# Moving the start-up work of a fused attention and gated-MLP kernel: one load queue, an earlier copy, later transposes, no power function on GpSimd

## The chip, the cores and the metric

The kernel runs on one NeuronCore of one Trainium2 chip. The metric is device microseconds of one execution, as the median of several; lower is better. Besides the time, each execution has a *span*: from the first to the last instruction that the profile records. The time is longer than the span.

In the profile the engines are PE (TensorE matmuls), PEld (TensorE weight loads), DVE (VectorE), ACT (ScalarE), POOL (GpSimd) and SP (SyncE, which here only issues DMAs). A "q" behind a name means the engine's sequencer, for instance the time in which it issues a DMA.

## The reference

The input x is normalised once (layer norm without scale), and two branches use the result: a sliding dilated local attention and a gated bilinear MLP. Cut to what matters:

```python
# x: 2048 x 640 bf16; 32 heads of 20; window 8, dilation 2; F = 1536
xn  = (x - mean) / sqrt(var + 1e-5)
qkv = xn @ wqkv                              # 640 x 1920
attn over the 8 keys at pos, pos-2, ..., pos-14
A   = attn_output @ wo
B   = ((xn @ w_gate) * (xn @ w_up)) @ w_down
return x + A + B
```

## The kernel before

Every operation goes through a small scheduler: the program calls `op(engine, ...)` in one sequence, each engine runs its share in that order, and the scheduler adds the semaphore waits. So the order of the calls is the order on each engine; nothing is reordered.

The sixteen row tiles of x (128 x 640) are loaded, normalised and transposed. Tiles 0 to 3 are transposed by TensorE and copied out of PSUM, tiles 4 to 15 by DMA ("transposing loads" below). Q and K of tiles 0 to 3 are projected tile by tile with 128-wide matmuls, of tiles 4 to 7 with 256-wide ones, and everything after that with 512-wide ones.

The loads, alternating between the queues of SP and ScalarE:

```python
    x_load(1, "act")
    x_load(0)
    for c in range(NCH):                                  # NCH = 5: the Q weights
        wqkv_load(0, c, ("sp", "act")[c % 2])
    x_load(2, "act")
    x_load(3)
    for c in range(NCH):                                  # the K weights
        wqkv_load(1, c, ("sp", "act")[c % 2])
    for t in range(4, 8):
        x_load(t)
```

The layer norm of tile t. For tiles 8 to 15 the reciprocal root comes from GpSimd:

```python
    def ln_aggr(t):
        ...
        op("dve", ... bn_aggr(mv, st) ...)                # mean, variance
        if t >= 8:
            op("pool", ... tensor_scalar(sd, mv[:, 1:2], EPS, None, op0=ALU.add) ...)
            op("pool", ... tensor_tensor(rstd, sd, NEGH[:, 0:1], ALU.pow) ...)   # NEGH = -0.5
            return
        op("act", ... activation(sd, mv[:, 1:2], ACT.Sqrt, bias=EPSC[:, 0:1]) ...)

    def ln_apply(t):
        ...
        if t < 8:
            op("dve", ... reciprocal(rstd, sd) ...)
        op("dve", ... tensor_scalar(xs, x, mean, rstd, subtract, multiply) ...)
        if t >= NTP:                                      # NTP = 4
            op("sp", ... dma_start_transpose(XNT tile t, xs) ...)
        if t + 8 < NT:
            x_load(t + 8)
```

The start. `warm` issues matmuls on zeros, `ln_pe` the five PE transposes of a tile, `ln_copy` the copies of the transposed tile from PSUM to SBUF (half by ScalarE, half by VectorE for tiles 0 and 1):

```python
    warm(10)
    ln_stats_a(0); ln_stats_b(0); ln_aggr(0)
    ln_stats_a(1)
    ln_apply(0)
    ln_pe(0)
    ln_stats_b(1)
    ln_aggr(1)
    ln_copy(0)
    ln_apply(1)
    ln_stats_a(2)
    warm(2)
```

The transposes of tiles 1 to 3 are put between the projections' groups of five matmuls, one group for each of the five row blocks c of the weights. The key is (Q or K, tile), the value the group ahead of which the transpose stands:

```python
    at = {(0, 0): (3, lambda: tr(1)), (0, 1): (4, lambda: tr(2)), (1, 1): (2, lambda: tr(3))}
```

## Time and profile before

| | before |
|---|---|
| time | 255.28 us (255.06 to 255.30, 3 runs) |
| span of the profiled execution | 253.7 us (that execution took 255.53 us) |
| PE busy | 249.7 us, 98% |
| first projection matmul / first 512-wide one | 6.72 / 30.48 us |
| last matmul begins | 251.12 us |

From the page of before: the span, the engines' busy times, and the engines' shares of the chain that ended last.

```profile
span 253.7 us, 3853 instructions
PE 249.7 (98%) x1573; PEld 149.3 (59%) x1573; DVE 216.5 (85%) x241; ACT 112.9 (45%) x202; POOL 47.0 (19%) x73
PE 95%; DMA 2%; DVE 1%; ACTq 0%; ACT 0%; issue 0%
```

PE sets the time. Its waits in the whole execution of before (who waited for whom: us in total, times, longest):

```profile
PE PS L420 <- DVE EPSC L298: 1.0, 1, 1.0
PE PS L403 <- DVE XNS L389: 0.3, 1, 0.3
PE PS L468 <- ACT XNT L414: 0.2, 1, 0.2
```

The first is the wait before the very first matmul. The other two, about 0.5 us, are all that PE loses later: the transposes of tile 2 wait for its normalised rows (XNS), and the first projection waits for ScalarE's copy of transposed tile 0 (XNT). The chain of waits of before says why tile 2 is late (start, us, what):

```profile
2.36 5.57 DMA XST<-in_A_x_dram
...
7.95 0.49 DVE STATS L358
8.45 0.19 DVE XNT L412
8.63 0.41 DVE STATS L364
...
9.84 0.46 DVE XNS L389
10.30 0.05 issue
10.34 0.45 PE PS L403 x5
```

Tile 2's load is issued at 2.36 us and lands at 7.93; VectorE's in-order chain of statistics and normalisation follows. VectorE's copy of transposed tile 1 (8.45) also stands behind that load. From 10.34 us to the last matmul the chain is PE alone.

The power function, in the timelines of GpSimd and VectorE of before (start, us, what, and in brackets the idle time before it and who ended it):

```profile
21.73 0.22 POOL L373 TENSOR_SCALAR SD<-MV 128x1 f32<-128x1 f32 x1 [1.22 <-DVE MV L370]
22.03 0.58 POOL L374 TENSOR_TENSOR SD<-SD,NEGH 128x1 f32<-128x1 f32 x1
22.64 0.45 DVE L389 TENSOR_SCALAR XNS<-XST,MV,SD 128x640 bf16<-128x640 bf16 x1 [0.65 <-POOL SD L374]
```

VectorE waits for GpSimd in each of these eight tiles, 5.5 us in total (0.65 us here, 1.0 us at the last). PE does not wait for that.

```profile
q1 hardware_dynamic: 144, 0.04, 4.2%
q14 instruction: 1, 0.01, 0.8%
```

### The profile page before, as it was taken

The numbers are of one execution on the slowest core, as the hardware profiler recorded it, in microseconds if no ns is written. First come the engines' busy times: TensorE is split into PE (matmuls) and PEld (weight loads), VectorE is DVE, ScalarE is ACT, GpSimd is POOL, SyncE is SP. The second block draws the span as 40 slices with busy tenths as digits, with TensorE's granted clock in tenths as the row PEclk, the third lists the DMA queues.
The fourth block names the chain that finished last, engine by engine and source line by source line (L and its number), as shares of the span: only waits on it lengthen the run. The fifth ranks groups of instructions, "written<-read, shape, count | busy, mean of one in ns | idle before, by whom it ended". The sixth has DMA issues, their size and how long they took to land.

```text
span 253.7 us, 3853 instructions
## 1 busy us (share of the span) xinstructions
PE 249.7 (98%) x1573; PEld 149.3 (59%) x1573; DVE 216.5 (85%) x241; ACT 112.9 (45%) x202; POOL 47.0 (19%) x73
## 2 busy tenths in 40 slices
PE   8999999999999999999999999999999999999996
PEld 3899955555554444444444447764444777777775
DVE  5896679999999994999999994899999999995221
ACT  3575557555555557555555553325555112211000
POOL 2003320113453252002232102120000112112000
PEclk9999999999999999999999999999999999999999
DMA  6959448967866546364469962393000042332311
GB/s 213 332 117 170 82 79 303 375 178 142 138 127 110 106 83 125 114 238 90 75 117 253 393 230 24 51 314 68 3 0 0 4 50 26 36 45 26 80 52 52
DMA packets 25665, 31.84 MB, mean 126 GB/s; under 512 B 10000, under 2 KB 22160, under 8 KB 25616
## 3 DMA queue, kind: packets, MB, share of 16 engines
q1 hardware_dynamic: 18448, 21.31, 26.7%
q0 software_dynamic: 6336, 9.31, 23.7%
q10 hardware_dynamic: 864, 0.98, 1.2%
q8 instruction: 12, 0.20, 0.3%
q14 instruction: 5, 0.04, 0.0%
HBM read 14.42 MB, written 4.59 MB: 75 GB/s over the span
## 4 chain that ended last, share of the span: by engine, by line
PE 95%; DMA 2%; DVE 1%; ACTq 0%; ACT 0%; issue 0%
PE PS L614 41%; PE PS L645 29%; PE PS L442 17%; PE PS L475 4%; PE PS L457 2%; DMA XST<-in_A_x_dram 2%; PE PS L468 1%; DVE STATS L358 0%; ACTq L294 0%; PE PS L403 0%; ACT L321 0%; DVE XNS L389 0%; DVE STATS L364 0%; DVE FOUT L654 0%; DVE MV L370 0%
## 5 line engine op out<-in xcount | busy, mean ns | idle before, releaser
L614 PE MATMUL PS<-XNT,WG 128*128 128x512 bf16 x240 | 59.6, 379 | 0.0
L614 PE MATMUL PS<-XNT,WU 128*128 128x512 bf16 x240 | 59.6, 379 | 0.0
L581 DVE TENSOR_TENSOR PVB<-VO,ATB 128x10240 f16<-128x10240 bf16 x8 | 43.9, 5489 | 0.2
L442 PE MATMUL PS<-XNT,WQKV 128*128 128x512 bf16 x200 | 43.3, 379 | 0.0
L645 PE MATMUL PS<-WD,HT 128*128 128x320 bf16 (+1 forms) x300 | 43.2, 294 | 0.0
L614 PEld LDWEIGHTS PS<-XNT,WU 128*128 128x128 bf16 x240 | 23.5, 98 | 28.3
L614 PEld LDWEIGHTS PS<-XNT,WG 128*128 128x128 bf16 x240 | 23.5, 98 | 28.2
L616 ACT ACTIVATE USX<-PS 128x512 bf16<-128x512 f32 x48 | 28.7, 597 | 22.6 <-PE PS L614 22.2
L645 PEld LDWEIGHTS PS<-WD,HT 128*128 128x128 bf16 x300 | 28.7, 98 | 10.9
L442 PEld LDWEIGHTS PS<-XNT,WQKV 128*128 128x128 bf16 x200 | 23.5, 118 | 19.4
L576 DVE TENSOR_TENSOR PVB<-PVB 128x5120 f16<-128x5120 f16 (+1 forms) x16 | 34.5, 2156 | 0.3
L509 POOL DMA_DIRECT2D LOG<-PE x24 | 22.5, 937 | 57.6 <-DMA LOG<-PE 57.4
L649 ACT ACTIVATE FACC<-PS 128x320 f16<-128x320 f32 x24 | 10.5, 437 | 41.9 <-PE PS L645 41.9
L616 ACT ACTIVATE HT<-PS 128x512 bf16<-128x512 f32 x36 | 21.5, 597 | 16.5 <-PE PS L614 16.5
L645 PE MATMUL PS<-WO,VO 128*128 128x320 bf16 (+1 forms) x165 | 27.1, 295 | 0.0
L660 POOL DMA_DIRECT2D out_dram<-FACC x12 | 10.4, 865 | 71.2 <-ACT FACC L649 71.2
L645 PEld LDWEIGHTS PS<-WO,VO 128*128 128x128 bf16 x165 | 15.9, 98 | 5.9
L498 DVE TENSOR_TENSOR TMP<-QH,KH 128x2048 f16<-128x2048 bf16 x16 | 19.1, 1218 | 0.0
L498 DVE TENSOR_TENSOR PP<-QH,KH 128x2048 f16<-128x2048 bf16 x16 | 18.9, 1218 | 0.0
L503 DVE TENSOR_TENSOR PP<-PP,TMP 128x4096 f16<-128x4096 f16 x8 | 18.3, 2291 | 0.2
L654 DVE TENSOR_TENSOR FOUT<-PS,XR 128x320 bf16<-128x320 f32 (+1 forms) x9 | 4.1, 455 | 15.8 <-PE PS L645 15.8
L449 ACT ACTIVATE VO<-PS 128x512 bf16<-128x512 f32 x20 | 11.9, 597 | 9.6 <-PE PS L442 9.6
(65 smaller groups left out, 227.8 us busy)
## 6 DMA issues: line engine op xcount, KB each, us to landing
PE<-PP POOLq DMA_DIRECT2D x8, 512.0 KB, 4.8
ATB<-LOG SPq DMA_DIRECT2D x8, 512.0 KB, 4.3
LOG<-PE POOLq DMA_DIRECT2D x24, 128.0 KB, 2.7
XST<-in_A_x_dram SPq DMA_DIRECT2D x14, 160.0 KB, 4.7
WG<-in_B_w_gate_dram SPq DMA_DIRECT2D x1, 1920.0 KB, 9.4
WU<-in_B_w_up_dram SPq DMA_DIRECT2D x1, 1920.0 KB, 16.1
WD<-in_B_w_down_dram SPq DMA_DIRECT2D x1, 1920.0 KB, 10.3
out_dram<-in_A_x_dram SPq DMA_DIRECT2D x1, 1920.0 KB, 10.1
```

The lines of the kernel that those rows point to most:

```text
L442: op("pe", (lambda l, x, c: lambda e: e.matmul(PS[:, b, :], l, x, start=(c == 0), stop=(c == NCH - 1)))(l, x, c), r=[l, x], w=[PS[:, b, :] ...
L449: op("act", lambda e: e.activation(o, PS[:, b, :], ACT.Copy, scale=sc), r=[PS[:, b, :]], w=[o], name=f"pev{which}_{m}_{j}")
L498: return (1.22, lambda: op("dve", lambda e: e.tensor_tensor(o, qw, kw, ALU.mult), r=[q, k], w=[o], name=f"prod{h}_{p}_{c}"))
L503: (2.3, lambda: op("dve", lambda e: e.tensor_tensor(a, a, b, ALU.add), r=[a, b], w=[a], name=f"psum{h}_{p}")),
L509: op("pool", lambda e: e.dma_start(o, i, accum_op=ALU.add), r=[o, i], w=[o], dma=True, name=name)
L576: return lambda: op("dve", lambda e: e.tensor_tensor(o, x, y, ALU.add), r=[x, y], w=[o], name=f"{name}_{b}")
L581: lambda: op("dve", lambda e: e.tensor_tensor(PVB[:], vw, aw, ALU.mult), r=[v, a], w=[PVB[:]], name=f"pv_{b}")),
L614: op("pe", (lambda l, x, c: lambda e: e.matmul(PS[:, b, :], l, x, start=(c == 0), stop=(c == NCH - 1)))(l, x, c), r=[l, x], w=[PS[:, b, :] ...
L616: op("act", lambda e: e.activation(o, PS[:, b, :], ACT.Copy), r=[PS[:, b, :]], w=[o], name=f"guev{which}_{m}_{j}")
L645: op("pe", (lambda l, x, i, b: lambda e: e.matmul(PS[:, b, 0:wid], l, x, start=(i == 0), stop=(i == n - 1)))(l, x, i, b), r=[l, x], w=[PS[ ...
L649: op("act", (lambda o, b: lambda e: e.activation(o, PS[:, b, 0:wid], ACT.Copy))(o, b), r=[PS[:, b, :]], w=[o], name=f"fin{t}_{nb}")
L660: stores.append(op("pool", lambda e: e.dma_start(d, f, accum_op=ALU.add), r=[f, ("out",)], w=[("out", t)], dma=True, name=f"oacc{t}"))
```

## The change

Four edits, meant to shorten the first 11 us and to free GpSimd of the small operations of layer norm: (1) all weight loads and tile 2 on SP's queue; (2) ScalarE's copy of transposed tile 0 ahead of the Sqrt of tile 1, which waits for statistics; (3) the PE transposes of tiles 1 to 3 later among the projections; (4) no pow: tiles 8 to 15 use ScalarE's Sqrt and VectorE's reciprocal, as tiles 0 to 7 do.

```diff
-    NEGH = sb("NEGH", [128, 16], FP32)
-    op("pool", lambda e: e.memset(NEGH[:], -0.5), w=[NEGH[:]], name="negh")
     for c in range(NCH):
-        wqkv_load(0, c, ("sp", "act")[c % 2])
-    x_load(2, "act")
+        wqkv_load(0, c)
+    x_load(2)
     x_load(3)
     for c in range(NCH):
-        wqkv_load(1, c, ("sp", "act")[c % 2])
+        wqkv_load(1, c)
@@ ln_aggr
-        if t >= 8:
-            rstd = SD[:, t, 1:2]
-            op("pool", ... tensor_scalar ... add ...)
-            op("pool", ... tensor_tensor ... pow ...)
-            return
@@ ln_apply
-        if t < 8:
-            op("dve", lambda e: e.reciprocal(rstd, sd), ...)
+        op("dve", lambda e: e.reciprocal(rstd, sd), ...)
@@ ln_copy gets an argument `only`, to emit one engine's copy alone
@@ start
     ln_pe(0)
+    ln_copy(0, "act")
     ln_stats_b(1)
     ln_aggr(1)
-    ln_copy(0)
+    ln_copy(0, "dve")
@@ projections
-    at = {(0, 0): (3, lambda: tr(1)), (0, 1): (4, lambda: tr(2)), (1, 1): (2, lambda: tr(3))}
+    at = {(0, 0): (4, lambda: tr(1)), (1, 0): (3, lambda: tr(2)), (1, 1): (4, lambda: tr(3))}
```

More of the change, by code (lines that the diff above doesn't have):

```diff
@@ L370, in ln_aggr @@
         op("dve", lambda e: e.bn_aggr(mv, st), r=[st, ("stb", t)], w=[mv], name=f"bnag{t}")
-        if t >= 8:
-            rstd = SD[:, t, 1:2]
-            op("pool", lambda e: e.tensor_scalar(sd, mv[:, 1:2], EPS, None, op0=ALU.add), r=[mv], w=[("sd", t)], name=f"sd{t}")
-            op("pool", lambda e: e.tensor_tensor(rstd, sd, NEGH[:, 0:1], ALU.pow), r=[("sd", t), NEGH[:]], w=[("rstd", t)],
-               name=f"rstd{t}")
-            return
         op("act", lambda e: e.activation(sd, mv[:, 1:2], ACT.Sqrt, bias=EPSC[:, 0:1]), r=[mv, EPSC[:]], w=[("sd", t)],
@@ L384, in ln_apply @@
         sd, rstd = SD[:, t, 0:1], SD[:, t, 1:2]
-        if t < 8:
-            op("dve", lambda e: e.reciprocal(rstd, sd), r=[("sd", t)], w=[("rstd", t)], name=f"rstd{t}")
+        op("dve", lambda e: e.reciprocal(rstd, sd), r=[("sd", t)], w=[("rstd", t)], name=f"rstd{t}")
         for c0, c1 in ((0, 2 * 128), (2 * 128, D)) if t == 0 else ((0, D),):
@@ L403, in ln_pe, with ln_copy @@
             op("pe", (lambda o, i: lambda e: e.transpose(o, i, IDENT[:]))(o, i), r=[i, IDENT[:]], w=[o], name=f"tr{t}_{c}")
-    def ln_copy(t):
+    def ln_copy(t, only=None):
         parts = ((("act", 0, 2), ("dve", 2, NCH)), (("dve", 0, 2), ("act", 2, NCH)), (("act", 0, NCH),),
@@ L408, in ln_copy @@
         for eng, c0, c1 in parts:
+            if only is not None and eng != only:
+                continue
             o = XNT[:, c0:c1, t * TS:(t + 1) * TS]
```

## The prediction

> **What bounds it.** TensorE: busy 98% of the 253.7 us span, clock granted in full; the chain of waits is 95% PE. From tile 2's transposes at 10.34 us to the last matmul at 251.36 that chain is PE without a wait, so only the first 11 us can give anything back. PE's waits there: 0.98 us before the warming matmuls, 0.18 us on ScalarE's copy of transposed tile 0 (first projection matmul at 6.72), 0.34 us on VectorE's normalised tile 2 (10.00 to 10.34). The weight-load row adds 0.26 us (until 8.69) behind VectorE's copy of tile 1, about 0.2 us for PE. Together 0.7 us.
>
> Tile 2 is late because its statistics wait for its x load, issued at 2.36, landed at 7.93, eighth to land. The DMA share is 1.0 (340 to 380 GB/s) from 5 to 10.8 us: bandwidth-bound, not issue-bound.
>
> **What the change does.**
> - *One queue.* An issue costs 0.43 to 0.46 us, so thirteen on SP end near 6.7 us instead of 4.9. The landing order (two x tiles, five Q weights, tiles 2 and 3, K weights) is already that of the trace. [...]at 164 KB per 0.455 us (360 GB/s) one queue nearly keeps up. Tile 2 lands at 7 to 8 us.
> - *Copy before second Sqrt.* ScalarE's copy starts when its transposes end, near 5.6 instead of 6.30; PE's 0.18 us wait goes. But VectorE's copy of tile 1 sits behind tile 2's statistics, so if tile 2 still lands at 7.93, the wait ending near 8.69 grows by as much.
> - *Later transposes.* Tile 2's go behind 20 more matmuls (0.057 us each): the 0.34 us wait vanishes. Tile 1's behind five more: 0 to -0.1. Tile 3's behind ten more: copied near 14.0, needed near 15.
> - *No pow.* Sixteen GpSimd instructions (224 and 569 ns) go; eight Sqrt on ScalarE (0.29 us) and reciprocals on VectorE (0.16 us) come. VectorE's tile period falls from 2.09 to 1.65 us (the 0.64 us waits on GpSimd go), so layer norm ends about 3.5 us earlier, near 32. PE does not wait for that. ScalarE's evacuations now stand behind Sqrts paced by VectorE and lag up to 3.5 us; with eight PSUM banks filled at 1.09 us each, over 2 us remain before PE would stall. Tile 11's transposing load lands near 27.5 instead of 29.7, which keeps the other gains from being eaten.
>
> **Sum.** PE reaches the 200 wide-row matmuls 0.5 us earlier (0.3 to 0.8). All after that is PE-paced and moves as a block.
>
> Predicted 254.7 us, 80% range 253.9 to 255.5. Chances: faster by over 2% 0.01, within 2% 0.97, slower 0.02.
>
> **Right if:** no PE wait on ScalarE's copy near 6.6 nor on tile 2's normalisation; 512-wide projections start near 30.0 instead of 30.48; VectorE's first 2048-wide product near 32 instead of 35.55; PE's busy time per group equal; ScalarE waits more on VectorE's statistics, without a PE wait from it. A remaining PE wait near 8.5 on VectorE's copy shows whether tile 2 landed sooner.
>
> **Wrong if:** one queue delivers clearly slower (tile 2 or K weights after 9 or 10 us: PE waits on WQKV), or ScalarE's lag exhausts the PSUM banks (PE waits on ScalarE between 20 and 40 us): up to 2 us slower. Or earlier VectorE work shifts the DMA accumulations and stalls PE later.

Cut from the step *One queue* is a statement about several issuing queues that no run here shows. It was no term of the sum: the sum, 0.5 us (0.3 to 0.8), and the 254.7 us made from it are whole. What carries that step is the estimate from the trace, 164 KB per 0.455 us of issue, against a mean of 362 GB/s that the DMA of before moved from 5 to 10.8 us.

## More of the kernel before

One view that I looked at only afterwards belongs here as well: the DMA queues in two stretches of before. First 140 to 149 us, then 252 to 256 us, which is the very end. Queues q8 and q14 carry instruction fetches; the columns are packets, MB, and the packets' time as a share of 16 DMA engines.

```profile
q8 instruction: 1, 0.02, 0.7%
q14 instruction: 2, 0.02, 0.4%
```

## The result, and the profile after

| | before | after |
|---|---|---|
| time, median | 255.22 us (255.06 to 255.34, 6 runs) | 255.38 us (255.32 to 259.66, 6 runs) |
| span of the profiled execution | 253.7 us | 253.0 us |
| first 512-wide matmul | 30.48 us | 29.77 us |
| last matmul begins | 251.12 us | 250.40 us |

The ratio is 1.0009, with a 95% interval from 0.9996 to 1.0023: the same. Ratios here are the mean time of one kernel's fast runs over that of the other's of the same rounds, so they are not quite the ratio of the medians quoted. One of the six runs of after (259.66 us, clock 0.993) was slow and is left out.

The page of after, the same lines:

```profile
span 253.0 us, 3850 instructions
PE 249.6 (99%) x1573; PEld 149.6 (59%) x1573; DVE 218.1 (86%) x249; ACT 114.0 (45%) x210; POOL 41.0 (16%) x56
PE 99%; DVE 0%; issue 0%
```

PE's waits of after, all of them:

```profile
PE PS L413 <- DVE EPSC L297: 1.0, 1, 1.0
```

The chain of waits of after, from the start into the tile-wise projections, has PE alone. (The chain counts a piece from the end of the one before it, so its times lie a little behind the starts quoted elsewhere: 6.83 us here, 6.62 us in the timeline.)

```profile
0.99 4.45 PE PS L413 x10
5.44 0.53 PE PS L394 x5
5.98 0.85 PE PS L413 x2
6.83 1.12 PE PS L461 x20
7.95 0.28 PE PS L394 x5
8.23 2.65 PE PS L461 x45
```

Inside the span of this execution nearly everything went as foreseen: both waits are gone, PE has no wait after its first matmul, and all that follows is 0.7 us earlier (predicted 0.5, within 0.3 to 0.8). VectorE's layer norm ends at 32.0 us, where it ended at 35.6. In the timelines of ScalarE and VectorE of after, ScalarE's evacuations now stand behind a Sqrt that waits for VectorE, and they lag; for that reason VectorE's first product of the attention starts at 33.37 us and not at 32 as I had written:

```profile
24.43 0.29 ACT L369 ACTIVATE SD<-MV,EPSC 128x1 f32<-128x1 f32 x1 [0.87 <-DVE MV L368]
24.64 0.36 ACT L476 ACTIVATE QH<-PS 128x256 bf16<-128x256 f32 x1
33.37 1.23 DVE L491 TENSOR_TENSOR PE<-QH,KH 128x2048 f16<-128x2048 bf16 x1 [1.35 <-ACT KH L476]
```

PE does not wait for any of it. And yet the time is not shorter. The profiled execution of after took 255.32 us with a span of 253.0, a difference of 2.3 us; that of before took 255.53 us with 253.7, a difference of 1.8. The six runs of after all have 2.26 to 2.34 us. So about half a microsecond had appeared *outside* the span. That was the question for the experiments.

### The profile page after: what moved, and what is told of

It reads as the page before. It is cut to its first block, busy times and chain, and to the rows that moved or that the text cites. A ratio compares the mean times of both kernels' runs of the same rounds, so it can differ in the third digit from the quotient of the medians.

```text
span 253.0 us, 3850 instructions
## 1 busy us (share of the span) xinstructions
PE 249.6 (99%) x1573; PEld 149.6 (59%) x1573; DVE 218.1 (86%) x249; ACT 114.0 (45%) x210; POOL 41.0 (16%) x56
## 4 chain that ended last, share of the span: by engine, by line
PE 99%; DVE 0%; issue 0%
PE PS L607 41%; PE PS L638 29%; PE PS L435 17%; PE PS L468 4%; PE PS L461 2%; PE PS L450 2%; PE PS L413 2%; PE PS L394 1%; DVE FOUT L647 0%; DVE ZERO L296 0%; DVE EPSC L297 0%
## 5 line engine op out<-in xcount | busy, mean ns | idle before, releaser
L502 POOL DMA_DIRECT2D LOG<-PE x24 | 21.9, 925 | 58.4 <-DMA LOG<-PE 58.1
```

The source lines that it names most:

```text
L502: op("pool", lambda e: e.dma_start(o, i, accum_op=ALU.add), r=[o, i], w=[o], dma=True, name=name)
```

## The experiments

All ran in five rounds against before on the same chip. "Copy", "slots", "queue" and "pow" are the four edits. Runs of one table block share the runs of before. The spans are to 0.1 us, so only the first decimal of "time minus span" counts.

| run | what it is | time, median | ratio, 95% interval | spans of its runs | time minus span |
|---|---|---|---|---|---|
| *(before, first)* | 11 runs | 255.65 | | 253.2 to 254.8 | 1.77 to 1.88, one 2.09 |
| c_before | before again | 255.78 | 0.9995 (0.9976 to 1.0014) | 253.3 to 254.1 | 1.76 to 1.82 |
| c_after | after again | 255.55 | 1.0007 (0.9983 to 1.0032) | 253.1 to 254.8 | 2.23 to 2.28 |
| e_twoq | after, two queues | 255.44 | 0.9992 (0.9970 to 1.0014) | 252.5 to 254.0 | 2.27 to 2.34 |
| e_pow | after, with pow | 254.80 | 0.9986 (0.9954 to 1.0019) | 252.8 to 255.1 | 1.76 to 1.83 |
| *(before, second)* | 11 runs | 255.32 | | 253.2 to 254.0 | 1.78 to 1.85 |
| p4_gps | after + 4 idle GpSimd memsets | 256.36 | 1.0031 (1.0012 to 1.0050) | 253.3 to 255.2 | 1.74 to 1.83 |
| p17_dve | after + 17 idle VectorE memsets | 255.31 | 0.9998 (0.9985 to 1.0011) | 252.8 to 253.2 | 2.27 to 2.31 |
| o_nopow | before, pow removed | 256.10 | 1.0030 (1.0018 to 1.0042) | 253.7 to 254.0 | 2.27 to 2.30 |
| p4_twoq | e_twoq + 4 idle GpSimd memsets | 254.92 | 0.9984 (0.9971 to 0.9997) | 252.8 to 253.6 | 1.77 to 1.82 |
| *(before, third)* | 11 runs | 255.41 | | 253.3 to 254.0 | 1.76 to 1.85 |
| o_oneq | before, one queue | 255.19 | 0.9989 (0.9977 to 1.0001) | 253.2 to 253.6 | 1.74 to 1.84 |
| o_slots | before, later slots | 254.84 | 0.9977 (0.9964 to 0.9990) | 252.9 to 253.7 | 1.76 to 1.84 |
| o_copy | before, early copy | 255.63 | 1.0006 (0.9994 to 1.0018) | 253.2 to 254.2 | 1.79 to 1.86 |
| b_cs | before, copy and slots | 255.01 | 0.9984 (0.9972 to 0.9995) | 252.9 to 253.6 | 1.76 to 1.84 |

### First call: is the lost half microsecond real, and whose is it?

**c_before and c_after.** No edit; they give the spans of timed runs of both kernels on one chip.

> Control: the kernel before, unchanged, so that the span of its own timed runs is known (so far only that of one profiled execution is, 253.7 us at a time of 255.53 us). Theory A (the 0.7 us gained inside the span is real, and something outside the span, about 0.5 us, takes it back): timed runs near 255.2 us with spans near 253.4, so time minus span near 1.8 us. Theory B (the one profiled execution of before was an unlucky one, with a late x tile 2, and its timed runs hardly wait): spans near 253.0 and time minus span near 2.2 us, as in the changed kernel, whose six runs show 2.3.

> Control: the changed kernel, unchanged, on the same chip. Both theories: 255.3 to 255.4 us, spans 253.0 to 253.1, time minus span 2.3 us, last matmul near 250.7 us in the trace. If the ratio to before comes out at 0.998 or below here, the earlier verdict (1.0009) was a matter of chip or noise.

Theory A holds in its main point: time minus span is 1.8 us for before and about 2.25 us for after, in all runs but one of before (2.09), though c_before ran longer than expected (medians of 255.78 us and of 254.0 us for the span, not 255.2 and 253.4). Theory B fails: spans near 253.0 us did not come. But on this chip the spans vary by a microsecond from run to run, so a single profiled execution says little about a gain of 0.5 us. The median span is 253.8 us for the eleven runs of before and 253.3 for after, a gain of 0.5 us inside the span; two runs of after had long spans, 254.4 and 254.8 us, to which I come back.

**e_twoq.** The edit puts the loads back on two queues:

```diff
-        wqkv_load(0, c)
-    x_load(2)
+        wqkv_load(0, c, ("sp", "act")[c % 2])
+    x_load(2, "act")
...
-        wqkv_load(1, c)
+        wqkv_load(1, c, ("sp", "act")[c % 2])
```

> The changed kernel with the weight loads back on two queues; the early copy, the later slots and the removed pow stay. Theory A, with the second queue as the cause of the lost half microsecond: time near 254.8 us, span near 253.0. Theory B or any other cause outside the span: same time as the changed kernel within 0.2 us. By my prediction the queue itself is worth about 0, so the span is 252.9 to 253.3 in any case.

Time minus span stayed at 2.3 us. The queue is not the cause.

**e_pow.** The edit puts the `if t >= 8` branch of the kernel before, with NEGH and its memset, back into the changed kernel.

> The changed kernel with the GpSimd pow back for tiles 8 to 15; one queue, early copy and later slots stay. My prediction says that then tile 11's transposing load lands only just before the 512-wide projections need it, so the span grows by 0 to 0.3 us against the changed kernel. Theory A, with the GpSimd instructions or the longer in-order chain on ScalarE as the cause outside the span: time falls to near 254.8 us although the span does not. Theory B: time as the changed kernel or up to 0.3 us longer.

Time minus span fell to 1.8 us in all six runs, and four of them took 254.56 to 254.89 us. The expected growth of the span by a late tile 11 did not come (252.8 to 253.1 us in those four). The other two had spans of 254.9 and 255.1 us. So with the GpSimd pow, which in before costs 6.3 us of busy time on GpSimd and makes VectorE wait 5.5 us, the part of the time that lies outside the span is half a microsecond *shorter*.

### Why removing work adds time: the instruction fetch

The DMA records of the traces include the fetches of the instructions themselves, 8192 bytes each on queue q14 (and, in before and after, twelve of 16,384 bytes each on q8). On q14 in before, after the start, they begin at 25.3, 36.7, 141.5, 146.7, 150.5 and 254.8 us. In after they begin at 22.8, 36.0, 126.1, 149.5, 253.0 and 254.0 us. I counted how many recorded instructions each engine had begun at each fetch. The one at 146.7 us in before comes when GpSimd has begun 68 of its 85; the one at 145.5 us in e_pow also comes at GpSimd's 68th. After has only 68 recorded GpSimd instructions in all, closing ones included, and has no such fetch in mid-kernel but one more around the end. The same two stretches of after, as shown of before (140 to 149 us, then 252 to 256 us):

```profile
q1 hardware_dynamic: 523, 3.19, 94.3%
q0 software_dynamic: 108, 0.11, 7.3%
q8 instruction: 1, 0.02, 0.7%
```

```profile
q14 instruction: 2, 0.02, 1.6%
q1 hardware_dynamic: 53, 0.01, 1.4%
```

In the first stretch these are all the queues of after: q14 has no fetch where before had two (of before's two, the one at 141.5 us is VectorE's, which has moved to 126.1 us, see p17_dve). In the last stretch it has two where before had one. The theory, an inference from these two kernels and e_pow: one of GpSimd's fetches comes at its 68th recorded instruction. With the pow that is in mid-kernel (146.7 us in before, where PE waits for nothing after 10.34 us), and time minus span is 1.8 us; without it the fetch falls at the end, and time minus span is 2.3 us, 0.5 us more.

Two cautions belong to this. In before GpSimd's count stays at 68 from 141.8 to 152.0 us, so the count alone does not single out the fetch at 146.7 us; the experiment p4_gps does. And before, too, has a fetch 1.06 us after the end of its span, with 1.8 us outside the span. So not every fetch out there costs half a microsecond, and why GpSimd's should is not shown.

**p4_gps.** The test: four GpSimd memsets that nobody reads, at 2.5 us, where GpSimd is idle (30.9 us on end in after).

```diff
+    PADT = sb("PADT", [128, 4, 16], FP32)
...
+    for n in range(4):
+        op("pool", (lambda n: lambda e: e.memset(PADT[:, n], 0.0))(n), w=[PADT[:, n]], name=f"pad{n}")
```

> The changed kernel with four dead memsets on GpSimd near 2.5 us, where GpSimd idles for 30 us; nothing reads them. Theory F (fetch): the time minus span, 1.8 us with pow and 2.3 us without[...]: in the trace of before an 8192-byte instruction fetch begins at 146.7 us when GpSimd has run 68 instructions; without the pow GpSimd has only 68 in all, that fetch is missing in mid-kernel and two are seen around the end. Then four idle instructions move it back inside: time minus span 1.8 us, time near 254.9 us (spans 253.1), 0.5 us faster than the changed kernel. Rival (the work itself: eight Sqrt and reciprocals more, or what GpSimd last did): 2.3 us stays, time near 255.4.

Time minus span fell from 2.3 to 1.8 us in all six runs, as the theory said. In its trace the fetch is back inside, at 231.4 us, and again at GpSimd's 68th instruction, now of 72: it begins 0.17 us after that instruction has ended (0.19 us in p4_twoq, at 229.1 us). Around the end there is one fetch again, not two. The DMA queues of p4_gps from 228 to 235 us:

```profile
q0 software_dynamic: 244, 0.27, 31.5%
q14 instruction: 1, 0.01, 0.4%
```

But the time missed the expectation by 1.5 us (256.36 instead of 254.9): five of six spans were 254.1 to 255.2 us. That is another matter, inside the span, and is treated below.

**p17_dve.** Seventeen such memsets on VectorE instead (the same edit with `"dve"` and 17, at 1 us).

> The changed kernel with seventeen dead memsets on VectorE near 1 us, where it waits for the first x tile until 3 us. Theory F with GpSimd as the engine: no help, time minus span stays 2.3 us, time near 255.4. If VectorE's or the total number of instructions is what counts, time minus span changes here too; the fetch near 126 us should move to another time by VectorE's seventeen.

Time minus span stayed at 2.3 us. The fetch at 141.5 us in before and 126.1 us in after moved to 102.4 us: it belongs to VectorE, which has 266, 274 and 291 recorded instructions in the three kernels, so here more instructions went with an earlier fetch (not at one recorded count, though: it comes at the 189th, 185th and 174th; why is open). Of these two engines only GpSimd's count changes the time outside the span. ScalarE's and SP's counts differ as well, between one queue and two (260 and 84 in after, 265 and 79 in e_twoq), and both have 2.3 us.

**o_nopow.** The kernel before with the pow branch, NEGH and its memset removed, nothing else.

> The kernel before with the GpSimd pow alone removed; two queues, late copy, early slots stay. If removing pow is what costs 0.5 us outside the span, time minus span is 2.3 us and time 0.5 us above before (ratio 1.002) with the span of before, as TensorE never waited for the pow. If it needs the other parts too, time minus span is 1.8 us and the ratio 1.000.

Time minus span is 2.3 us, and the ratio is 1.0030: removing the pow alone costs 0.77 us (0.0030 of 255.4; 0.5 to 1.1 us by the interval). Half a microsecond of it lies outside the span. Its mean span is 253.86 us against 253.59 for before in the same rounds; what the other 0.27 us is, if it is not noise (the spans of before alone range over 0.8 us), I have not found out.

**p4_twoq.** The four GpSimd memsets in the two-queue variant.

> The changed kernel with the weight loads on two queues and four dead GpSimd memsets. Theory F: time minus span 1.8 us, time 0.5 us below that of the two-queue variant without the memsets, near 254.7 to 254.9. Against the one-queue kernel with the same memsets this measures the queue alone; my prediction says about 0 (within 0.2 us).

Time minus span is 1.8 us, as expected, and the time 254.92 us, ratio 0.9984. That the whole time fell by 0.5 us is not shown by this: e_twoq ran on another chip, and measured against before in their own rounds the two differ by 0.0008 (0.2 us), well within their intervals. The comparison with p4_gps, which was to measure the queue, came out at 0.0047 and not at 0.

### The long spans of some one-queue runs

Kernels with one queue and the later slots show spans of 254.4 us or more in some runs: two of six of c_after, two of six of e_pow, four of six of p4_gps; none of five of p17_dve and none of the five fast runs of after's first set. The two-queue variants show none above 254.2 us, and before itself one (254.8) in 33 runs. The profiled execution of p4_gps is one of the long ones. Its waits of PE:

```profile
PE PS L471 <- DMA XNT<-XNS: 1.6, 1, 1.6
PE PS L416 <- DVE EPSC L298: 1.0, 1, 1.0
PE PS L464 <- DVE XNT L408: 0.5, 1, 0.5
PE PS L397 <- DVE XNS L383: 0.4, 1, 0.4
```

The 1.6 us is the first 256-wide matmul waiting for the transposing load of tile 5. In SP's queue that load stands behind the x load of tile 12 (the timeline of SP of p4_gps, DMA issues):

```profile
14.68 1.34 SPq L387 DMA_TRANSPOSE XNT<-XNS  x1
16.07 0.57 SPq L294 DMA_DIRECT2D XST<-in_A_x_dram  x1
16.70 1.22 SPq L387 DMA_TRANSPOSE XNT<-XNS  x1
```

The transposing load of tile 4 is issued at 14.68 us (13.87 in after), since x tile 4 landed only at 11.93 us (11.12 in after). The x load of tile 12, issued at 16.07, landed at 20.28 us, 4.2 us later (in after 15.25 to 18.03, 2.8 us), and the transposing load of tile 5 landed at 20.92 us (18.77). The trace shows a part of the reason: on queue q1, packets that begin from 18.60 us on last 0.8 us or more, and the last of them ends at 20.31. Every one of the fourteen traces has such a stretch (2 to 22 packets) between 18.6 and 22.0 us (19.65 to 21.21 in before, where x tile 13 and tile 6's transposing load take 4.2 us each and PE does not wait). In the other thirteen it begins 0.5 to 1.0 us after tile 5's transposing load has landed; in p4_gps, where that load was issued 0.8 us later than in after, it fell on it. What causes the stretch, and why x tile 4 is late in some runs only, is not shown. Whether the unprofiled long runs have the same cause is open.

**o_oneq.** One queue alone, in the kernel before (the reverse of e_twoq's edit).

> The kernel before with the weight loads on one queue, nothing else. My prediction: about 0 in time and span, time minus span 1.8 us. Rival, from the one-queue runs so far: x tile 4 lands 0.4 to 1.6 us later on one queue (10.6 to 11.9 us against 10.2 to 10.6), and some runs have spans 1.5 to 2 us longer (two of six of the changed kernel, two of six with the pow back, most of those with four memsets), as TensorE then waits for tile 5's transposing load ahead of the 256-wide projections. Then some of these runs show spans of 254.5 or more, or the median span is at least 0.3 above before's.

The rival misses: no span above 253.6 us, and the ratio is 0.9989, so one queue alone does no harm and is perhaps worth 0.3 us. In its trace x tile 2 landed at 7.32 us instead of 7.93, within the 7 to 8 us of the prediction. One queue is therefore not harmful by itself; the long spans need the later slots or the early copy as well, or are chance. I leave that open.

### Which part brings the gain?

**o_slots.** The line `at = {...}` of the diff alone.

> The kernel before with the transposes in their later slots, nothing else. My prediction gives this part nearly all of the gain: span 0.3 to 0.5 us below before's of the same rounds, time minus span 1.8 us, ratio 0.998 to 0.999; the trace has no TensorE wait on the normalised tile 2. The 0.18 us or more on ScalarE's late copy stays.

Ratio 0.9977: this part alone is worth 0.6 us (0.0023 of 255.46, the mean of before), a little more than predicted, and it is the best ratio. Its profiled execution was the slowest of its runs (span 253.7, the others 252.9 to 253.4) with x tile 2 landing at 8.46 us, and even there no wait on the normalised tile 2 is left. PE's waits of o_slots:

```profile
PE PS L420 <- DVE EPSC L298: 1.0, 1, 1.0
PE PS L468 <- DVE XNT L412: 0.6, 1, 0.6
```

The wait that remains is on VectorE's copy of tile 1, which stands behind the statistics of tile 2.

**o_copy.** The early copy alone.

> The kernel before with the first copy ahead of the second Sqrt, nothing else. My prediction: about 0, since TensorE then only waits longer for VectorE's copy of tile 1 or for the normalised tile 2, both behind x tile 2's landing. Rival: the two waits add, and the span falls by 0.2 to 0.5 us (0.5 was the wait on that copy in the second trace of before).

Ratio 1.0006: nothing measurable. In its trace the first projection matmul starts at 6.36 us instead of 6.72, and then PE waits for VectorE. PE's waits of o_copy:

```profile
PE PS L422 <- DVE EPSC L298: 1.0, 1, 1.0
PE PS L470 <- DVE XNT L414: 0.6, 1, 0.6
PE PS L403 <- DVE XNS L389: 0.3, 1, 0.3
```

The gain turned into a longer wait for the same thing, x tile 2; the rival (the waits add) falls.

**b_cs.** Copy and slots together, two queues, pow kept.

> The kernel before with early copy and later slots; two queues and the pow stay. This is the version to which the runs point: no exposed fetch (time minus span 1.8 us), no late x tile 4. Time near 254.7 (254.5 to 254.9), ratio 0.997 to 0.998, spans 252.7 to 253.1, below both kernels and at or just below the two-queue variant with four memsets.

It beats before (255.01 us, ratio 0.9984), and through that comparison after, which did not run in these rounds; but by less than I expected (254.7), and it is no better than the slots alone: their intervals overlap widely. The early copy adds nothing measurable even there; in its trace PE waits 0.9 us for VectorE's copy of tile 1.

The four parts taken alone sum to -0.0011 - 0.0023 + 0.0006 + 0.0030 = +0.0002, 0.05 us. The whole change measured +0.0009 and +0.0007 in its two sets. Each part is uncertain by about 0.0012, so the agreement is loose, but it fits this account: the slots, and perhaps the queue, bring 0.6 to 0.9 us, and the removed pow takes it back.

## Why the prediction was right or wrong

The time, 255.38 us, lies in the range (253.9 to 255.5) and "within 2%" was right. But the expected value of 254.7 us was 0.7 us too low, for the most part because one term of its sum was missing: 0.5 us outside the span. The rest is a gain inside the span that was smaller in the timed runs than in the profiled one: before's spans there can be estimated at 253.4 us (255.22 less 1.8), and after's fast runs had 253.0 to 253.5. That the range held is luck in part: it was wide enough upwards (0.8 us) for a cost that nobody had foreseen.

- *What bounds it* was right: PE, with only the first 11 us to gain.
- *Later transposes* was right: the wait on tile 2 disappears in after and in o_slots, and o_slots alone gains 0.6 us.
- *Copy before second Sqrt* was right: ScalarE's copy starts at 5.69 us and its wait goes, but PE then waits for VectorE's copy of tile 1 (0.6 us in o_copy). Alone it is worth nothing measurable.
- *One queue* was about right in size (0.9989 alone, predicted about 0; tile 2 landed at 7.03 us in after and 7.78 in c_after, predicted 7 to 8). The warning sign "clearly slower" came in a form I had not thought of: long spans in some runs of the one-queue kernels with the other parts.
- *No pow* is the step that failed. I wrote that sixteen GpSimd instructions go, that VectorE's tile period falls to 1.65 us, that layer norm ends near 32 us and that PE does not wait for it. All of this is what the trace shows. The step priced the removal at zero, because it looked only at what waits inside the span. The runs showed +0.5 us of time minus span in all five sets of runs with so short a GpSimd program (after, c_after, e_twoq, p17_dve, o_nopow), and 1.8 us again as soon as GpSimd had four instructions more, idle ones included.
- *"All after that ... moves as a block"* was right for the span and wrong for the time, for the same reason.
- *VectorE's first product near 32 us* was wrong: 33.37. I had priced ScalarE's lag for PE (no stall, right), but not that VectorE's own next step needs ScalarE's evacuations.

What is shown and what is argued: that the number of GpSimd instructions decides about the 0.5 us is shown for the counts that ran (68 against 72 and 85), by p4_gps and p4_twoq against after and e_twoq. That the exposed fetch is what costs it is supported by all fourteen profiled executions (the fetch at GpSimd's 68th instruction is in mid-kernel or near 230 us where the difference is 1.8 us, and missing there, with one more around the end, where it is 2.3), but what GpSimd executes after its 68th, its last recorded instruction, lies outside the recorded span, so the wait for the fetch is not seen directly.

The size of a gain inside the start also depends on something that I took as fixed. The ten warming matmuls step at 0.43 us each and later at 0.22; the step changes after about 4.2 us in the trace of c_before (in c_after it is 0.22 from 4.29 us on) but only after 6.2 us in that of after. That is about 3 us and more than 5 us after the first matmul; what sets the moment is not shown. In after the first projection therefore started at 6.62 us, in c_after at 6.15 (even after a wait of 0.35 us for the normalised tile 0, which its faster warming had run into), and c_after then lost the lead in waiting for VectorE's copy of tile 1 (0.6 us). Both reached the 512-wide matmuls within 0.3 us of each other.

## What to carry to other kernels

When a change shortens the span in the profile and the time does not follow, compare time minus span of both kernels first: here 0.5 us of the cost (2.3 us against 1.8) lay outside everything that the profile records. With 68 recorded GpSimd instructions instead of 85, a fetch that before has in mid-kernel (146.7 us) was missing there and one more came around the end (253.0 and 254.0 us in after, 254.8 us alone in before); that this fetch costs the 0.5 us is the theory that these runs support, and its wait was not seen. Four idle GpSimd instructions took the 0.5 us outside the span away again; that they make the whole time shorter is not shown here (0.9992 without and 0.9984 with them on two queues, 1.0007 and 1.0031 on one). In o_copy a wait of 0.2 us was removed ahead of another wait on the same late load, and PE waited 0.6 us for that one instead (ratio 1.0006); moving the consumer later, as the transposes in o_slots (0.9977), is what paid.
